# Reordering the start of an attention and MoE kernel: one w_in half ahead of V's last pair, reciprocals spread by TensorE, second tile's transposes and casts rearranged

## The chip, the cores and the metric

The kernel runs on one NeuronCore of a Trainium2 chip. The metric is the device time in microseconds (us); the span of the profile is some 1.8 us shorter than it. Ratios are the mean time of one kernel's fast runs over that of the kernel before in the same rounds, so they are not quite the ratios of the medians.

## The reference

```python
# attention in chunks of 64 keys: B = H = 8, S = 576, D = 64
scores = (1/sqrt(D)) * q_c @ k_c.T          # within each chunk
attn   = softmax(scores)
out    = attn @ v_c
# MoE: x is the attention's output as 4608 x 512
g   = gelu_exact(x @ w_in)                  # 512 x 2048
out = g @ w_out                             # 2048 x 512
```

## The kernel before

The 4608 tokens are worked in nine tiles of 512. A tile's attention (T: transposes of q and k, S: scores, U: sums and reciprocals, A: the product with V, called AV, and x = AV times reciprocal; each in four pairs of heads, 0 to 3) lies inside the matmuls of the tile ahead of it: the h products (x w_in, followed by Gelu) and then the y products (with w_out). From the second tile on, U is one step for all four pairs: sums on TensorE, a transpose and reciprocals on VectorE, 16 small copies on ScalarE (rb), then one more transpose per pair. Only the first tile has nothing in front of it. The start is therefore written out by hand, in the order in which each engine's queue gets its work:

```python
        load_v(0)                                             # eight transfers of 128 KB
        win = [load_w_in(c, 2 if c == 0 else 1) for c in range(NWC - 1)]
        # ... casts of q, k; all eight casts of V on GpSimd (PO); transposes; scores ...
        u2 = att_sum(0, 2, later=True)      # sum on TensorE, transpose, reciprocal, transpose on VectorE
        p3 = att_sum_pe(0, 3)               # sum and reciprocal small; p3() spreads it by 16 f32 matmuls
        u2()
        A[0]()
        p3()
        A[1]()
        act_table(Act.Gelu)
        keep_warm(1)
        A[2]()
        keep_warm(1)
        A[3]()
        # ...
        for i, eng in enumerate((PO, PO, DV, PO)):            # the first w_in quarter's four casts
            win[0](i, eng)
```

The spread:

```python
        def spread():
            rc_ps = ps_mm.tile([P, MT], f32, tag="mm", name="rc_ps")
            for m in range(MT // P):
                for r in range(2):
                    nc.tensor.matmul(rc_ps[CH * r:CH * (r + 1), m * P:(m + 1) * P],
                                     rr[:, m, r:r + 1].to_broadcast([P, D]), ident_f[:], ...)
            nc.scalar.copy(rc[:].rearrange("p n e -> p (n e)"), rc_ps[:])
```

The second tile's attention lies in the 16 slots of the first tile's second product (y = h w_out, four matmuls per slot):

```python
        for c in range(2, NWC):
            for i in range(FC):
                wout[c](i, PO)                                # GpSimd casts of w_out, then of V
        # ...
        phase(0, {}, {0: [lambda: act_table(Act.Exp)],
                      3: [T[0]], 4: [T[2]], 5: [T[4]], 6: [T[6], T[1]], 7: [T[3]], 8: [T[5], S_[0]], 9: [T[7], S_[1], next_qk],
                      10: [S_[2], S_[3]], 11: [U[0], lambda: act_table(Act.Gelu)], 12: [U[1], A[0]], 13: [U[2], A[1]],
                      14: [U[3], A[2]], 15: [U[4], A[3]]}, halved=True)
```

Even T are q, odd T are k. Slot 8 is the first to need the third quarter of w_out.

The softmax here doesn't subtract the row's maximum and nothing guards it: scores larger than these inputs give would overflow.

## Time and profile before

| | before |
|---|---|
| time, median of 3 runs at first | 296.86 us (296.45 to 296.9) |
| span of the profile | 294.0 us |
| TensorE busy | 281.9 us, 96% |
| first h product of tile 1 | 17.8 us |
| first h product of tile 2 | 52.0 us |

A TensorE that is 96% busy leaves 12 us at most. By the stretches, 6.6 us of it lie before 53 us, 3.8 us in the last stage and the end, and no more than 0.5 us in any stage between. The change touches only the first part. The lines are in the prediction. The profile is of a run of 295.75 us, 1.1 us below the median of the three.

### The profile page before, as it was taken

How to read it: one execution, taken by the hardware profiler on the slowest of the kernel's cores; microseconds unless marked ns; L12 is line 12 of the kernel's file. 1: busy time of each engine (PE TensorE's matmuls, PEld its weight loads, DVE VectorE, ACT ScalarE, POOL GpSimd, SP SyncE). 2: the span in 40 equal slices, each digit the busy share in tenths (PEclk: the TensorE clock that was granted, in tenths of full speed). 3: DMA queues.
4: the chain of work that ended last, by engine and by line, in shares of the span. 5: the costliest groups of instructions: out<-in, count | busy, mean ns of one | idle time of the engine just before them, and what ended most of it. 6: DMA issues, size and time to landing. Idle time of an engine off the chain costs nothing.

```text
span 294.0 us, 4846 instructions
## 1 busy us (share of the span) xinstructions
PE 281.9 (96%) x1837; PEld 138.2 (47%) x1871; DVE 126.5 (43%) x201; ACT 177.1 (60%) x380; POOL 98.6 (34%) x138
## 2 busy tenths in 40 slices
PE   5799999999999999999999999999999999999995
PEld 2554453345544454445445544554454445444444
DVE  6877256261816081618251735163325432550011
ACT  3756667767746773676368637872686368637400
POOL 7859748508711640182006500650003800000000
PEclk9999999999999999999999999999999999999999
DMA  7999999899669615971497149903999760020032
GB/s 231 272 377 404 393 271 291 272 210 331 172 166 323 161 68 149 314 183 71 130 300 204 58 136 287 248 36 124 206 127 150 223 143 2 36 88 21 0 71 71
DMA packets 96359, 53.79 MB, mean 183 GB/s; under 512 B 68560, under 2 KB 88272, under 8 KB 96336
## 3 DMA queue, kind: packets, MB, share of 16 engines
q1 hardware_dynamic: 96176, 53.36, 66.3%
q8 instruction: 14, 0.23, 0.3%
q10 hardware_dynamic: 160, 0.13, 0.2%
q14 instruction: 9, 0.07, 0.1%
HBM read 36.70 MB, written 9.44 MB: 157 GB/s over the span
## 4 chain that ended last, share of the span: by engine, by line
PE 81%; DMA 7%; SPq 4%; POOL 3%; ACT 2%; issue 1%; DVE 1%
PE h_ps L293 37%; PE y_ps L310 37%; DMA arrival<-in_moe_w_out_dram 4%; DMA arrival<-in_moe_w_in_dram 3%; PE av_ps L261 2%; PE s_ps L178 2%; SPq L127 2%; SPq L112 1%; PE y_ps L328 1%; ACT rb L225 1%; POOL w_in_sb L373 1%; PE sums_ps L216 1%; POOL w_out_sb L381 1%; POOL v_bd L462 1%; ACT y_sb L314 0%
## 5 line engine op out<-in xcount | busy, mean ns | idle before, releaser
L310 PE MATMUL y_ps<-w_out_sb,h 128*128 128x512 bf16 x539 | 130.5, 379 | 1.0
L293 PE MATMUL h_ps<-x,w_in_sb 128*128 128x512 bf16 x564 | 125.8, 379 | 1.6 <-ACT h L296 0.3
L296 ACT ACTIVATE h<-h_ps 128x512 bf16<-128x512 f32 x144 | 85.7, 597 | 63.6 <-PE h_ps L293 63.5
L293 PEld LDWEIGHTS <-w_in_sb 128*128 128x128 bf16 x576 | 56.3, 98 | 69.6 <-issue 1.8
L310 PEld LDWEIGHTS <-h 128*128 128x128 bf16 x560 | 49.6, 98 | 50.0 <-issue 1.8
L170 DVE COPY k_bd<-k_t 64x512 bf16<-64x512 bf16 x56 | 35.6, 635 | 48.0 <-DMA k_t<-k_nat 47.0
L131 POOL CAST q_nat<-arrival 128x512 bf16<-128x512 f32 x32 | 20.9, 692 | 95.2 <-DMA arrival<-in_q_dram 69.0
L135 POOL CAST v_bd<-arrival 64x512 bf16<-64x512 f32 (+1 forms) x30 | 36.5, 1216 | 20.3 <-DMA arrival<-in_v_dram 11.4
L225 ACT COPY rb<-r 32x16 f32<-32x16 f32 x128 | 25.8, 202 | 16.2 <-DVE r L221 14.5
L314 DVE COPY y_sb<-y_ps 128x512 f32<-128x512 f32 x17 | 11.7, 687 | 36.9 <-PE y_ps L310 36.9
L219 DVE STREAM_TRANSPOSE t<-sums_ps 128x512 f32<-128x512 f32 x8 | 5.7, 718 | 50.3 <-PE sums_ps L216 50.3
L262 DVE TENSOR_TENSOR x<-av_ps,rc 128x512 bf16<-128x512 f32 x36 | 24.7, 690 | 3.4
L232 DVE STREAM_TRANSPOSE rc<-rb 128x512 f32<-128x512 f32 x32 | 22.5, 704 | 7.3 <-ACT rb L225 7.3
L397 ACT ACT_TABLE_LOAD x18 | 23.1, 1283 | 1.0 <-PEq L520 0.7
L131 POOL CAST k_nat<-arrival 128x512 bf16<-128x512 f32 x32 | 18.6, 618 | 11.6 <-DMA arrival<-in_k_dram 5.7
L261 PEld LDWEIGHTS <-v_bd 128*128 128x128 bf16 x288 | 12.8, 98 | 9.5 <-POOL v_bd L135 2.5
L314 ACT COPY y_sb<-y_ps 128x512 f32<-128x512 f32 x18 | 10.2, 588 | 8.4 <-PE y_ps L310 8.4
L261 PE MATMUL av_ps<-pT,v_bd 128*128 128x64 bf16 x288 | 14.3, 193 | 0.6 <-POOL v_bd L135 0.3
L181 ACT ACTIVATE pT<-s_ps 128x512 bf16<-128x512 f32 x28 | 14.7, 592 | 0.0
L178 PEld LDWEIGHTS <-k_bd 128*128 128x128 bf16 x224 | 10.4, 98 | 6.6
L178 PE MATMUL s_ps<-q_t,k_bd 128*128 128x64 bf16 x224 | 11.1, 193 | 0.0
L155 ACT COPY k_bd<-tp 64x512 bf16<-64x512 bf16 x12 | 6.9, 579 | 4.8 <-PE tp L142 4.7
(59 smaller groups left out, 104.7 us busy)
## 6 DMA issues: line engine op xcount, KB each, us to landing
arrival<-in_v_dram SPq DMA_DIRECT2D x72, 128.0 KB, 4.1
out_dram<-y_sb SPq DMA_DIRECT2D x32, 256.0 KB, 2.0
arrival<-in_q_dram SPq DMA_DIRECT2D x7, 1024.0 KB, 6.1
arrival<-in_k_dram SPq DMA_DIRECT2D x7, 1024.0 KB, 8.5
arrival<-in_moe_w_out_dram SPq DMA_DIRECT2D x4, 1024.0 KB, 12.8
arrival<-in_moe_w_in_dram SPq DMA_DIRECT2D x3, 1024.0 KB, 10.4
arrival<-in_q_dram SPq DMA_DIRECT2D x4, 256.0 KB, 3.9
arrival<-in_k_dram SPq DMA_DIRECT2D x4, 256.0 KB, 4.4
```

Of the source, the lines that this page charges most:

```text
L131: copy(st[nm][:, g].rearrange("p j r d -> p r j d"), st[nm + "f"][:, 2 * g:2 * g + 2])
L135: copy(v_bds[t % NV][sl, :, gs, sl].rearrange("p i g d -> p g i d"), tiles[t]["vf"][sl, gs])
L170: copy(k_bds[g][sl, :, sl].rearrange("p i (c j) -> p i c j", j=J), src[sl])
L178: nc.tensor.matmul(s_ps[:, i, :].rearrange("p (j c) -> p j c", j=J), k_bds[g][:, i, :], qt[:, i], start=True, stop=True)
L225: nc.scalar.copy(rb[QD * s:QD * (s + 1), g], r1[QD * g:QD * (g + 1), s // 2])
L232: nc.vector.transpose(rc[:], rb[:, g].to_broadcast([P, NB, 32]))
L261: nc.tensor.matmul(av_ps[:, i, :], v_bds[t % NV][:, i, g, :], st["pT", g][:, i, :], start=True, stop=True)
L262: nc.vector.tensor_tensor(st["x"][:, g, :], av_ps[:].rearrange("p i e -> p (i e)"), st["rc", g][:].rearrange("p n e -> p (n e)"), op=mybir ...
L293: nc.tensor.matmul(h_ps[a][:], w_in_sb[:, ks, (f + a) * P:(f + a + 1) * P], st["x"][:, ks, :], start=(ks == 0), stop=(ks == KS - 1))
L296: nc.scalar.activation(st["h"][:, f + a, :], h_ps[a][:], Act.Gelu)
L310: nc.tensor.matmul(y_ps[:], st["h"][:, f, ms * P:(ms + 1) * P], w_out_sb[:, f, :], start=(f == 0), stop=(f == FF - 1))
L397: nc.scalar.activation(act_scratch[:], rest[:, 0:1], func)
```

## The change

Its intent: let the first w_in half land earlier, since GpSimd waits for it; take pair 2's two transposes off VectorE; let the second tile's k transposes start earlier; and share casts between GpSimd and VectorE.

```diff
-        load_v(0)
-        win = [load_w_in(c, 2 if c == 0 else 1) for c in range(NWC - 1)]
+        load_v(0, range(G - 1))
+        win = [load_w_in(0, lambda: load_v(0, [G - 1])), *[load_w_in(c) for c in range(1, NWC - 1)]]
 ...
-        for g in range(G):
+        for g in range(G - 1):
             cast_v(0, 0, PO, slice(g, g + 1))
             cast_v(0, 1, PO, slice(g, g + 1))
+        for i in range(2):
+            win[0](i, PO)
+        cast_v(0, 0, PO, slice(G - 1, G))
 ...
-        u2 = att_sum(0, 2, later=True)
+        p2 = att_sum_pe(0, 2)
         p3 = att_sum_pe(0, 3)
-        u2()
         A[0]()
+        p2()
+        A[1]()
         p3()
-        A[1]()
         act_table(Act.Gelu)
         keep_warm(1)
         A[2]()
+        cast_v(0, 1, DV, slice(G - 1, G))
         keep_warm(1)
         A[3]()
 ...
-        for i, eng in enumerate((PO, PO, DV, PO)):
-            win[0](i, eng)
+        win[0](2, PO)
+        win[0](3, PO)
 ...   (GpSimd casts only the first two of w_out's last quarter)
-                      3: [T[0]], 4: [T[2]], 5: [T[4]], 6: [T[6], T[1]], 7: [T[3]], 8: [T[5], S_[0]], 9: [T[7], S_[1], next_qk],
+                      3: [T[0]], 4: [T[2]], 5: [T[4], T[6]], 6: [T[1], T[3]], 8: [T[5], S_[0]],
+                      9: [T[7], lambda: wout[3](2, DV), lambda: wout[3](3, DV), S_[1], next_qk],
```

More of the change, by code (lines that the diff above doesn't have):

```diff
@@ L117, in load_qk, with load_v @@
                     src[b, h0:h1, MT:S, :].rearrange("h (p j) d -> p h j d", j=J))
-    def load_v(t, rs=(0, 1)):
-        vf = tiles[t]["vf"] = stage_tile()[:].rearrange("p (g i d) -> p g i d", g=G, d=D)
-        for g in range(G):
-            for r in rs:
+    def load_v(t, gs=range(G)):
+        if "vf" not in tiles[t]:
+            tiles[t]["vf"] = stage_tile()[:].rearrange("p (g i d) -> p g i d", g=G, d=D)
+        vf = tiles[t]["vf"]
+        for g in gs:
+            for r in range(2):
                 if t < B:
@@ L364, with load_w_in @@
     FC = FF // NWC
-    def load_w_in(c, parts=1):
+    def load_w_in(c, between=None):
         raw = stage_tile()[:].rearrange("p (ks n) -> p ks n", ks=KS)
-        n = WC // parts
-        for a in range(parts):
-            nc.sync.dma_start(raw[:, :, a * n:(a + 1) * n], w_in_v[:, :, c * WC + a * n:c * WC + (a + 1) * n])
+        n = WC // (2 if between else 1)
+        for a in range(0, WC, n):
+            nc.sync.dma_start(raw[:, :, a:a + n], w_in_v[:, :, c * WC + a:c * WC + a + n])
+            if between and a == 0:
+                between()
         def cast(i, copy):
@@ L416 @@
         cast_qk(0, "k", 3, PO)
-        for g in range(G):
+        for g in range(G - 1):
             cast_v(0, 0, PO, slice(g, g + 1))
             cast_v(0, 1, PO, slice(g, g + 1))
+        for i in range(2):
+            win[0](i, PO)
+        cast_v(0, 0, PO, slice(G - 1, G))
         cast_qk(0, "q", 0, DV)
@@ L471 @@
             cast_qk(1, "k", g, DV)
-        for c in range(2, NWC):
-            for i in range(FC):
-                wout[c](i, PO)
+        for i in range(FC):
+            wout[2](i, PO)
+        for i in range(2):
+            wout[3](i, PO)
         for g in range(G):
```

## The prediction

> **What bounds the kernel now**
>
> I read the page first, then busy times by stretch, then the timeline of the first 18 us engine by engine, then the chain of waits from 41 to 54 us. Busy times by stretch (us; PE, PEld, DVE, ACT, POOL; granted clock, DMA share, GB/s):
>
> ```profile
> PE 281.9 (96%) x1837; PEld 138.2 (47%) x1871; DVE 126.5 (43%) x201; ACT 177.1 (60%) x380; POOL 98.6 (34%) x138
> ...
> 0.00:17.78 17.78, 12.69 (x126) 7.52 (x127) 14.07 (x27) 9.60 (x16) 13.50 (x35) 1.00 0.90 269
> 17.78:31.95 14.17, 13.89 (x62) 6.28 (x65) 9.44 (x13) 9.61 (x17) 11.44 (x13) 1.00 1.05 397
> 31.95:41.00 9.05, 9.00 (x70) 5.00 (x70) 3.23 (x7) 5.79 (x10) 4.96 (x10) 1.00 1.09 381
> 41.00:52.99 11.99, 10.77 (x96) 4.77 (x97) 7.60 (x13) 9.39 (x28) 9.54 (x17) 1.00 0.88 252
> 52.99:83.33 30.34, 29.88 (x192) 14.40 (x196) 12.20 (x21) 19.15 (x43) 14.86 (x17) 1.00 0.83 233
> ```
>
> TensorE is the bound. From 53 us on it has no idle left worth naming, and the change touches nothing there. So only two things can move the time: when the first tile's first h product starts (17.8 us), and how much TensorE loses between 41 and 53 us. Both lie in code that the diff edits. From 17.8 to 41 us the transfers run without a gap, at about 390 GB/s: what lands there is set by the order and number of the bytes.
>
> The start, on TensorE, VectorE and GpSimd (start, length, engine, instructions, idle before):
>
> ```profile
> 14.52 0.25 PE L240 MATMUL sT<-ones_r,pT 128*128 128x2 bf16 x4
> 14.64 0.39 PE L261 MATMUL av_ps<-pT,v_bd 128*128 128x64 bf16 x8
> 15.31 1.09 PE L249 MATMUL rc_ps<-ident_f,rr 128*64 128x128 f32 x16 [0.28 <-DVE rr L243]
> 16.33 0.41 PE L261 MATMUL av_ps<-pT,v_bd 128*128 128x64 bf16 x8
> 17.79 0.39 PE L293 MATMUL h_ps<-x,w_in_sb 128*128 128x512 bf16 x1
> 18.34 0.39 PE L293 MATMUL h_ps<-x,w_in_sb 128*128 128x512 bf16 x1 [0.17 <-POOL w_in_sb L373]
> ...
> 16.12 2.55 DVE L262 TENSOR_TENSOR x<-av_ps,rc 128x512 bf16<-128x512 f32 x4
> ...
> 17.12 1.91 POOL L373 CAST w_in_sb<-arrival 128x512 bf16<-128x512 f32 x3 [1.27 <-DMA arrival<-in_moe_w_in_dram]
> ```
>
> Here the reader sees that GpSimd was idle for 1.27 us until the first w_in half landed at 17.1, and that the h products wait for its casts. From 18.34 they run without a hole: the next stage starts at 31.95, which is 63 x 0.216 = 13.6 us later. One matmul earlier, 18.12, is thus the effective start of the 64.
>
> The chain of waits in 41 to 54 us (start, length, what):
>
> ```profile
> 40.97 0.57 POOL w_out_sb L381
> 41.54 0.04 issue
> 41.58 0.38 PE y_ps L310
> 41.96 0.24 PE tp L142 x4
> ...
> 43.67 0.41 PE s_ps L190 x8
> ...
> 44.94 0.44 PE sums_ps L216 x4
> ...
> 49.99 1.28 ACT L397
> ...
> 51.49 1.46 ACT y_sb L314 x3
> ```
>
> The second tile's first h product needs a PSUM bank that ScalarE frees with a y copy. ScalarE reaches that copy only after 16 small rb copies (3.44 us) and the Gelu table load, and it starts those when the sums of the second tile are there. So the sums (44.9) set the start of the next stage (52.0): 7.1 us, in which nothing but this chain counts.
>
> **What the Trainium skill says**
>
> "TensorE: Matmul & The Clock Gate", section "Step-by-step: what each phase is for": matmuls stay in program order and only weight loads are pulled ahead. The trace agrees (no matmul above is out of the kernel's order). Hence a late AV product holds every h product behind it, even with x and w ready.
>
> "DMA: Bandwidth & Descriptors", section "Queues, rings and completion order": each DMA engine consumes descriptors in ring order. The trace agrees: w_in half 1, issued at 11.3 behind V, landed 5.7 us later.
>
> "SBUF — State Buffer" gives VectorE and GpSimd a shared port pair, which it calls "Lock-allocated, exclusive, held for the full instruction" (section Terms). The trace fits: VectorE's 128x512 casts took 0.42 us where GpSimd was idle (at 36.6) and 0.72 us beside a GpSimd cast (at 18.58).
>
> "ScalarE: Activation LUTs", section "What ACT_TABLE_LOAD costs": 1283 ns. The trace has 1.28 us in both places where a table load matters here.
>
> **The change part by part**
>
> *1. w_in half ahead of V's last pair.* The half is issued two V transfers earlier, 2 x 0.65 = 1.3 us. I put its landing at 15.8 instead of 17.1, V's last pair at about 16.5 instead of 13.3. GpSimd finishes six V casts at 10.34 + 6 x 0.69 = 14.5, casts w_in 0 and 1 from 15.8 to 17.1, then half of V's last pair until 17.8. Taken alone the h products could start about 1 us earlier.
>
> *2. Pair 2's reciprocals by TensorE.* Removed from VectorE: two transposes and a reciprocal, 0.68 + 0.25 + 0.71 = 1.64 us, just ahead of x. Added: a reciprocal of 0.17, a ScalarE copy of 0.59, and on TensorE 16 f32 products which take 1.02 us of its order (15.31 to 16.33 above) in place of one sum of about 0.22. The order becomes A0, spread 2, A1, spread 3, A2, A3. With pT for pair 3 at 14.5 as before: A0 at 14.64, spread 2 from 14.9, A1 at 15.9, spread 3 from 16.15 to 17.15, a warming product, A2 at 17.4. Without any other wait A3 comes at 17.8 and h at 18.0, practically the old 18.12. So part 2 uses up what part 1 wins.
>
> *3. Half of V's last pair on VectorE, behind x of pair 2.* This is the step that decides. x 2 needs A2, whose results stand at 17.8, and takes 0.64: 18.45. Then the V cast, 0.43 to 0.75 depending on GpSimd's w_in casts at that time: 18.9 to 19.2. A3 waits for it, and h waits for A3, 0.05 for the semaphore and 0.24 for eight products: 19.2 to 19.5. x of pair 3 follows by 20.4, in time for its use nine matmuls after the start. Against 18.12 the stage starts 1.1 to 1.4 us later; I take 1.2.
>
> *4. Second tile.* The transposes keep their order and only move between slots: q of pair 3 one slot up, k of pair 1 one slot up. The last ones, k of pairs 2 and 3, stay in slots 8 and 9, so the product that leads to the sums is preceded by the same TensorE work. Packing them may cost 0.1, since k of pair 1 needs a PSUM buffer whose ScalarE copy (0.59 each, two in a row) is just ending. In slot 8 the old kernel lost 0.2 waiting for the w_out cast of 40.97 (the fourth y product of the slot came at 41.58 instead of 41.38); a stage that arrives 1.2 later doesn't lose it. Sums: +1.2 + 0.1 - 0.2 = +1.1.
>
> *5. Two w_out casts to VectorE.* GpSimd is freed of 2 x 0.57, so its eight V casts begin at 44.1 instead of 45.2. Today each AV waits for them (0.3 to 0.8 us of weight-load idle at each). But behind those waits stands the ScalarE chain, which ends at sums + 7.1 whatever TensorE does, so I book nothing. The two casts on VectorE (0.43 to 0.83 each) fit between its last k copy and the sums' transpose: 43.61 to 45.40, a gap of 1.79.
>
> Sum: about +1.1 us at the start of the second tile, and the rest unchanged: 296.86 + 1.1 = 298.0. I go a little below, 297.6, because every timing of part 3 is a sum of small pieces and a faster result is easier to imagine than a much slower one.
>
> **The rivals**
>
> *The start wins.* If V's last pair lands before 16 us and A2 comes earlier than I think, x 2 and the V cast finish by 17.8; h starts at about 17.6, 0.5 earlier. For it: GpSimd's 1.27 us idle is real, and VectorE loses 1.6 us of work. Against it: spreads 2 and 3 stand in TensorE's order before A2. Even then the w_out transfer that lands at 39.18 holds slot 8 (casts until 41.53), so little of it reaches the sums: 296.4 to 296.9.
>
> *The V casts are the real bound of 41 to 53 us.* If the freed GpSimd lets AV and the y products end 1 us earlier and ScalarE's queue follows, the second stage gains up to 1 us: 296.0 to 297.0. Against it: the rb copies run back to back from 46.54 to 49.98 with no wait on TensorE.
>
> *A transfer starves.* V's staging buffer is released near 19.2 instead of 15.9, and a w_out load waits for it. Against it: at 19 us some 8.4 MB are issued and, by the GB/s row, some 5.2 MB moved; 3.2 MB at 0.39 MB/us is an 8 us reserve. If I am wrong, w_out lands later and the loss is 1 to 3 us: 299 to 300.
>
> **Range and chances**
>
> Loss at the start 0 to 1.5 and gain in the second stage 0 to 1 give 296.1 to 298.9 for 8 in 10. A 2% change is 5.9 us, as much as a third of the whole start; no mechanism here is that large. Faster 0.01, same 0.97, slower 0.02.
>
> **What would show it**
>
> Right: the w_in casts start near 15.8; A3's weight load waits for a VectorE v_bd cast at about 19; the first h product at 19.2 to 19.5; sums near 46; ScalarE's rb copies and table load in the chain as before; from 53 us on an unchanged profile, shifted. Wrong: A3 not waiting for VectorE, h before 18.2, or ScalarE's y copies starting other than 6.5 us after the sums. The size would be wrong if x 2 starts before 17.5 or if the f32 spreads take other than 1.02 us each.

## More of the kernel before

The rounds of different experiments fell on different chips at different times; the kernel before had medians of 296.44, 296.79, 297.24 and 296.68 us in them. Kernels of different rounds are therefore compared by their ratios.

## The result, and the profile after

The changed kernel took 298.25 us (median of 6 runs, 297.3 to 298.97) against 296.44 (6 runs, 295.66 to 296.9): a ratio of 1.0062, with a 95% interval of 1.004 to 1.0085. It is 1.8 us slower, which is within 2%.

TensorE's timeline of the changed kernel's start, then VectorE's and GpSimd's (start, length, engine, instructions, idle before):

```profile
13.32 0.61 PE L192 MATMUL s_ps<-qT,k_bd 128*128 128x64 bf16 x8 [0.59 <-ACT k_bd L157]
...
14.75 0.59 PE L263 MATMUL av_ps<-pT,v_bd 128*128 128x64 bf16 x8
15.27 1.98 PE L251 MATMUL rc_ps<-ident_f,rr 128*64 128x128 f32 x16
17.18 0.49 PE L263 MATMUL av_ps<-pT,v_bd 128*128 128x64 bf16 x8
17.60 1.09 PE L251 MATMUL rc_ps<-ident_f,rr 128*64 128x128 f32 x16
...
18.85 0.40 PE L263 MATMUL av_ps<-pT,v_bd 128*128 128x64 bf16 x8
...
20.65 0.39 PE L263 MATMUL av_ps<-pT,v_bd 128*128 128x64 bf16 x8 [1.18 <-DVE v_bd L137]
20.88 0.38 PE L295 MATMUL h_ps<-x,w_in_sb 128*128 128x512 bf16 x1
...
19.36 0.69 DVE L264 TENSOR_TENSOR x<-av_ps,rc 128x512 bf16<-128x512 f32 x1 [0.96 <-ACT rc L255]
20.08 0.42 DVE L137 CAST v_bd<-arrival 64x512 bf16<-64x512 f32 x1
...
15.70 1.16 POOL L377 CAST w_in_sb<-arrival 128x512 bf16<-128x512 f32 x2 [1.20 <-DMA arrival<-in_moe_w_in_dram]
```

The w_in casts do start 1.42 us earlier (15.70 for 17.12). They are of no use. A0, spread 2, A1, spread 3, A2 stand in line on TensorE. A3 then waits 1.18 us for VectorE's V cast, which itself stands behind x of pair 2. The h products begin at 20.88, where 19.2 to 19.5 had been forecast.

A second sight is the length of equal work. Spread 2 took 1.98 us and spread 3 only 1.09; the scores' eight matmuls took 0.61 us here and 0.41 at the same place in the kernel before. TensorE was at half rate until about 17.2 us here, and only until 13.4 there.

The chain of waits further on (start, length, what):

```profile
46.55 0.86 PE y_ps L312 x4
47.41 0.44 PE sums_ps L218 x4
...
52.46 1.28 ACT L401
...
53.96 1.46 ACT y_sb L316 x3
...
55.46 1.90 PE h_ps L295 x8
```

The sums come at 47.4 instead of 44.9, and from there the chain has the length that it had before. Busy times by stretch (the same columns as in the prediction):

```profile
20.88:34.69 13.81, 13.81 (x70) 6.27 (x67) 9.13 (x11) 8.84 (x15) 11.23 (x13) 1.00 1.06 397
34.69:43.47 8.78, 8.78 (x70) 5.00 (x69) 2.81 (x6) 5.58 (x10) 4.55 (x8) 1.00 0.98 320
43.47:55.46 11.99, 10.55 (x103) 5.18 (x100) 8.78 (x14) 9.52 (x28) 8.86 (x15) 1.00 0.77 232
55.46:85.80 30.34, 30.09 (x197) 14.38 (x197) 12.18 (x21) 19.14 (x43) 13.38 (x16) 1.00 0.83 233
```

The last cuts were laid at the distances that they had in the kernel before (11.99 and 30.34), so that their lengths show nothing. What does is the events: from the sums to the next tile's first h product it is 7.15 us before (44.87 to 52.02) and 7.14 here (47.34 to 54.48), and by TensorE's timeline the third tile's first h product comes at 82.90 before and at 85.36 here, 2.46 us later; the sums were 2.47 later. What was lost was lost before the sums.

### The profile page after: what moved, and what is told of

It reads as the page before. It is cut to its first block, busy times and chain, and to the rows that moved or that the text cites. A ratio compares the mean times of both kernels' runs of the same rounds, so it can differ in the third digit from the quotient of the medians.

```text
span 296.4 us, 4921 instructions
## 1 busy us (share of the span) xinstructions
PE 285.5 (96%) x1890; PEld 141.0 (48%) x1890; DVE 125.8 (42%) x201; ACT 177.6 (60%) x381; POOL 96.9 (33%) x136
## 2 busy tenths in 40 slices
DMA packets 96360, 53.81 MB, mean 182 GB/s; under 512 B 68560, under 2 KB 88272, under 8 KB 96336
## 4 chain that ended last, share of the span: by engine, by line
PE 91%; ACT 4%; DVE 3%; issue 1%
PE h_ps L295 42%; PE y_ps L312 39%; PE av_ps L263 3%; PE s_ps L180 2%; PE y_ps L330 1%; PE tp L144 1%; ACT k_bd L157 1%; ACT rb L227 1%; PE rc_ps L251 1%; PE sums_ps L218 1%; PE s_ps L192 1%; ACT y_sb L316 0%; DVE k_bd L157 0%; ACT L401 0%; DVE q_nat L133 0%
## 5 line engine op out<-in xcount | busy, mean ns | idle before, releaser
L312 PE MATMUL y_ps<-w_out_sb,h 128*128 128x512 bf16 x560 | 133.6, 379 | 0.0
L137 POOL CAST v_bd<-arrival 64x512 bf16<-64x512 f32 (+1 forms) x29 | 35.8, 1235 | 20.9 <-PE h_ps L295 11.2
L263 PE MATMUL av_ps<-pT,v_bd 128*128 128x64 bf16 x288 | 14.6, 195 | 1.9 <-DVE v_bd L137 1.2
L316 ACT COPY y_sb<-y_ps 128x512 f32<-128x512 f32 x18 | 10.2, 586 | 8.4 <-PE y_ps L312 8.4
```

The source lines that it names most:

```text
L137: copy(v_bds[t % NV][sl, :, gs, sl].rearrange("p i g d -> p g i d"), tiles[t]["vf"][sl, gs])
L263: nc.tensor.matmul(av_ps[:, i, :], v_bds[t % NV][:, i, g, :], st["pT", g][:, i, :], start=True, stop=True)
L312: nc.tensor.matmul(y_ps[:], st["h"][:, f, ms * P:(ms + 1) * P], w_out_sb[:, f, :], start=(f == 0), stop=(f == FF - 1))
```

## What fourteen profiles have in common

The profiles of the two kernels and of the twelve experiments can be put into one table. "S" is the start of the scores of pair 3 in tile 1, with their length in brackets: 0.41 is full rate, 0.61 half rate. "w_out" is the start of GpSimd's casts for slot 8, which had been waiting for that transfer each time. All numbers are us, each from its kernel's timeline. A profile is of one run and need not be a typical one: those of e5, e7 and e8 are of the slowest run of their kernel, those of e0, e3 and e9 of the fastest. So spans are not compared here, but distances within a profile.

| profile | S | first h | S to h | w_out | sums, tile 2 | first h, tile 2 | span |
|---|---|---|---|---|---|---|---|
| before | 13.41 (0.41) | 17.79 | 4.38 | 39.24 | 44.87 | 52.02 | 294.0 |
| changed | 13.32 (0.61) | 20.88 | 7.56 | 39.92 | 47.34 | 54.48 | 296.4 |
| e0 changed, again | 14.31 (0.41) | 20.50 | 6.19 | 40.52 | 46.96 | 54.11 | 296.1 |
| e1 V cast earlier | 14.49 (0.61) | 20.79 | 6.30 | 41.91 | 47.54 | 54.69 | 296.6 |
| e2 pair 2 on VectorE | 13.86 (0.61) | 20.92 | 7.06 | 39.93 | 47.39 | 54.53 | 296.5 |
| e3 start only | 13.97 (0.41) | 20.26 | 6.29 | 41.07 | 46.71 | 53.86 | 295.8 |
| e4 second tile only | 14.09 (0.41) | 18.15 | 4.06 | 41.03 | 46.66 | 53.81 | 295.8 |
| e5 changed, table late | 14.18 (0.61) | 21.55 | 7.37 | 40.99 | 48.02 | 54.63 | 296.0 |
| e6 before, table late | 13.43 (0.61) | 18.62 | 5.19 | 39.59 | 45.22 | 53.55 | 295.0 |
| e7 e1 and e2 together | 14.18 (0.41) | 19.55 | 5.37 | 43.42 | 49.05 | 56.19 | 298.1 |
| e8 e4, table late | 14.39 (0.61) | 19.73 | 5.34 | 41.00 | 46.63 | 53.24 | 294.8 |
| e9 e8, sums a slot earlier | 13.49 (0.61) | 18.86 | 5.37 | 39.54 | 44.79 | 51.46 | 293.1 |
| e10 changed, warmer | 12.83 (0.41) | 20.57 | 7.74 | 41.02 | 47.04 | 54.19 | 296.1 |
| e11 spread 2 only | 14.56 (0.41) | 19.41 | 4.85 | 41.07 | 46.70 | 53.84 | 295.8 |

Three things can be read from it.

**The sums come at whichever is later: first h + 26.46 or w_out + 5.63.** In the changed kernel, e0, e2, e5 and e10 the first holds to 0.02 us (20.88 + 26.46 = 47.34; 20.50 + 26.46 = 46.96). In before, e1, e4, e6, e7, e8 and e11 the second does (39.24 + 5.63 = 44.87; 43.42 + 5.63 = 49.05). In e3 both are equal within 0.02. Only e9, which moves the sums, has its own number (first h + 25.93). So a late start is hidden as far as the w_out landing is late. This landing wandered from profile to profile, between 39.2 and 41.1 with the old start and between 39.9 and 43.4 with the new order of transfers. The means are 40.2 and 41.1 (40.8 without e7); whether the new order delays it can't be said from so few, and no run tested it. Before slot 8 the transfers ran without a gap at 394 to 401 GB/s from 24 to 40 us; what differed was the time from 8 to 17 us, where they moved 217 to 284 GB/s, and in e7 also that from 17 to 24 us (321 GB/s, the others 369 to 400).

**The rate of TensorE rose by chance early or late.** Six profiles without e10 have full rate at S (it rose between 12.8 and 14.6), seven don't and rise between 17 and 19 us. Both groups hold kernels with the old start and with the new one. The same kernel fell in both (changed, late; e0, early). "TensorE: Matmul & The Clock Gate", section "What's actually happening", tells of a window of 3413 ns that is free-running, so that it does not begin with the kernel; the two groups lie about such a window apart. A late rise costs either start about as much: S to h is 4.06 to 4.38 at early rise and 5.19 to 5.37 at late rise with the old start (before, e4; e6, e8, e9), 6.19 to 6.29 and 7.37 to 7.56 with the new one (e0, e3; e5, changed).

**Like for like, the new start takes 2.0 to 2.2 us longer.** From the means of those groups: 6.24 - 4.22 = 2.0 at early rise, 7.47 - 5.30 = 2.2 at late rise. So the half rate is not the cause of the loss, though comparing one profile with one would have made it seem so. The old start at early rise, from the TensorE timeline of e4 (scores, third AV and fourth AV, h), to be set beside e0 below:

```profile
14.09 0.41 PE L190 MATMUL s_ps<-qT,k_bd 128*128 128x64 bf16 x8 [0.64 <-ACT k_bd L155]
...
17.47 0.40 PE L261 MATMUL av_ps<-pT,v_bd 128*128 128x64 bf16 x8
...
17.92 0.40 PE L261 MATMUL av_ps<-pT,v_bd 128*128 128x64 bf16 x8
18.15 3.62 PE L293 MATMUL h_ps<-x,w_in_sb 128*128 128x512 bf16 x15
```

Here h follows A3 at once, and so it does in e6, e8, e9 and e11. Of the six profiles with the old order of transfers only the first one had h waiting for w_in.

## The experiments

**e1: the V cast behind x of pair 1.** Is it the cast's place in VectorE's queue that holds A3, or the transfer?

```diff
         A[1]()
+        cast_v(0, 1, DV, slice(G - 1, G))
         p3()
 ...
         A[2]()
-        cast_v(0, 1, DV, slice(G - 1, G))
```

> The changed kernel with VectorE's V cast moved from behind x of pair 2 to behind x of pair 1; nothing else. Theory 1 (the cast's place in VectorE's queue holds A3): A3 follows A2 directly at about 19.3 in the changed kernel's clock phase, the first h product comes 1.2 to 1.5 us earlier than its 20.9, and the time falls by 0.9 to 1.3 us, to 297.0 to 297.3. Rival (the late landing of V's last pair holds A3): VectorE then waits for the transfer and h and the time stay within 0.3 us of the changed kernel's 298.25.

Measured: 297.66 us, ratio 1.0029 (0.9992 to 1.0066), about 1 us less than the changed kernel's 1.0062, as theory 1 had it (the median itself lies above its 297.0 to 297.3, but so did the kernel before's in these rounds). In its TensorE and VectorE timelines A3 (the third line below) follows the warming product at once:

```profile
20.11 0.40 PE L263 MATMUL av_ps<-pT,v_bd 128*128 128x64 bf16 x8 [0.16 <-POOL w_in_sb L377]
20.34 0.38 PE L396 MATMUL warm<-rest,ident 128*128 128x512 bf16 x1
20.56 0.40 PE L263 MATMUL av_ps<-pT,v_bd 128*128 128x64 bf16 x8
20.79 2.54 PE L295 MATMUL h_ps<-x,w_in_sb 128*128 128x512 bf16 x11
...
19.68 0.57 DVE L137 CAST v_bd<-arrival 64x512 bf16<-64x512 f32 x1
```

The first line is A2. The cast is done at 20.25, before A2 ends. S to h is 6.30 against 7.37 to 7.56 at the same (late) rise: 1.2 us, as theory 1 said. What is left over the old start's 5.19 to 5.37 is 1.0 us, and spread 2 still stands there. That the first h stands at 20.79 all the same is because S stands 1.2 us later in this profile (14.49 for 13.32). The interval of the ratio is wide and overlaps that of the changed kernel; the trace carries the verdict.

**e2: pair 2's reciprocals back on VectorE**, with the V cast left behind x of pair 2.

```diff
-        p2 = att_sum_pe(0, 2)
+        u2 = att_sum(0, 2, later=True)
         p3 = att_sum_pe(0, 3)
+        u2()
         A[0]()
-        p2()
-        A[1]()
         p3()
+        A[1]()
```

> The changed kernel with pair 2's reciprocals back on VectorE as before; the V cast stays behind x of pair 2. Theory 1 (spread 2 costs TensorE's order 1.0 us at full clock, 1.9 at half clock, and A2 stands behind it): A2 comes 1.0 to 1.9 us earlier, x of pair 2 and the V cast with it, so h starts 0.9 to 1.9 earlier and the time falls by 0.6 to 1.6 us, to 296.7 to 297.6. Rival (VectorE's 1.6 us of transposes were the bound of the start, so giving them back costs): h starts later or equal and the time is 298.2 or more.

Measured: 297.92 us, ratio 1.0040 (1.0015 to 1.0066), so 0.65 us less than the changed kernel, at the low end of what theory 1 allowed. The two intervals overlap, so the time alone does not bring the rival down; the trace speaks against it, and e11 below does. In the trace A2 comes 0.9 us earlier after S (18.49 - 13.86 = 4.63 against 5.53), but only 0.5 of it reaches h: x of pair 1 now waits behind the one spread that is left, at half rate 1.88 us, and the V cast still stands behind x of pair 2 (A3 waited 1.59 us for it).

**e3: the changed start with the old second tile**, and **e4: the old start with the changed second tile.** The edits swap the block of w_out casts and the slot table shown above.

> The changed start alone, with the second tile as before. Theory 1 (all of the loss is in the start; the second tile's part is worth 0 to 0.4): 298.2 to 298.7, and sums of the second tile at start of h plus 26.3 to 26.9 as in both kernels. Rival (the second tile's part gains about 1 us, or loses): 299 or more, or 297.5 or less.

> The second tile's changes alone, with the start as before. Theory 1 (ScalarE's chain behind the sums is the bound there, the freed GpSimd is of no use): 296.2 to 296.7, within 0.3 us of before; AV products no longer wait for GpSimd's V casts, yet h of the second tile starts 7.1 us after the sums as before. Rival (the V casts were the bound): 295.3 to 295.9, h less than 6.5 us after the sums.

Measured: e3 299.03 us, ratio 1.0080 (1.0052 to 1.0108), 0.3 us above what was expected and by its number in the rival's range (299 or more), though the kernel before was 0.35 us higher in these rounds too; e4 296.98 us, ratio 1.0007 (0.9978 to 1.0035). The loss lies in the start, and the second tile's part alone moves nothing that can be measured. In e4 first h minus sums is 53.81 - 46.66 = 7.15 us, the same as before. That no AV product would wait for GpSimd did not come true there: its last w_out quarter was cast from 44.89 on, and the weight loads of all four AV products wait for V casts, 1.7 us in sum (2.5 before). In the changed kernel and in e0 none does, and there too h comes 7.14 and 7.15 us after the sums. Whether the second tile's part takes back a little of a late start (1.0080 for e3, 1.0062 and 1.0052 for the whole change) can't be said within these intervals.

**e0: the changed kernel again**, as a control for the next three.

> The changed kernel once more, unaltered, as a control beside the next three and as a second profile of its start. Theory 1 (the loss is in the changed start, on average 1.2 to 2 us): 0.4 to 0.7% above before. What the profiles so far suggest besides: the matmuls change from 0.61 to 0.40 us (groups of eight 128x64) at a time that differs from run to run, 13.4 to 14.0 in some and 17.2 to 18.8 in others, and w_out for slot 8 lands between 39.2 and 41.9. If that is chance and not the change, this profile may show any of these, with spread 2 at 1.0 us when the rise is early and 1.9 when late.

Measured: 298.97 us, ratio 1.0052 (1.0026 to 1.0078). Its profile fell in the early rise. From its TensorE timeline:

```profile
14.31 0.41 PE L192 MATMUL s_ps<-qT,k_bd 128*128 128x64 bf16 x8 [0.59 <-ACT k_bd L157]
15.53 0.39 PE L263 MATMUL av_ps<-pT,v_bd 128*128 128x64 bf16 x8
15.86 1.09 PE L251 MATMUL rc_ps<-ident_f,rr 128*64 128x128 f32 x16
16.88 0.41 PE L263 MATMUL av_ps<-pT,v_bd 128*128 128x64 bf16 x8
17.22 1.09 PE L251 MATMUL rc_ps<-ident_f,rr 128*64 128x128 f32 x16
18.47 0.40 PE L263 MATMUL av_ps<-pT,v_bd 128*128 128x64 bf16 x8
20.27 0.39 PE L263 MATMUL av_ps<-pT,v_bd 128*128 128x64 bf16 x8 [1.18 <-DVE v_bd L137]
```

This is the prediction's order with its durations: 1.02 us from spread to the next AV (15.86 to 16.88), and the wait of A3 for VectorE. Only the whole lies 0.9 us later, because S does.

**e7: e1 and e2 together**, so that of the new start only the transfer order and the shared casts are left.

> The changed kernel with pair 2's reciprocals on VectorE as before and the V cast behind x of pair 1; left of the changed start are the transfer order and the shared V and w_in casts. Theory 1 (A3 late through spread 2 and the V cast, nothing else): the whole loss of the start is gone, within 0.3 us of before (0.999 to 1.001). Rival (the transfer order itself costs, because the second w_in half lands later or V's last pair holds A3): 0.6 us or more above before.

Measured: 297.76 us, ratio 1.0029 (0.9998 to 1.006). A miss: 0.9 us were left, where theory 1 had none and the rival 0.6 or more. In its TensorE and GpSimd timelines:

```profile
19.31 0.41 PE L263 MATMUL av_ps<-pT,v_bd 128*128 128x64 bf16 x8 [1.14 <-POOL v_bd L137]
...
17.34 1.17 POOL L377 CAST w_in_sb<-arrival 128x512 bf16<-128x512 f32 x2 [1.75 <-DMA arrival<-in_moe_w_in_dram]
18.45 0.80 POOL L137 CAST v_bd<-arrival 64x512 bf16<-64x512 f32 x1
```

A3 now waits 1.14 us for the other half of V's last pair. GpSimd's queue has it behind the two w_in casts, and these wait for w_in, which in this run landed at 17.3. In the other profiles with the new order where the casts were read they start between 15.0 and 17.3. So the new order carries a second wait of its own: A3 needs what stands behind w_in in one queue. Where w_in lands as in the changed kernel (that V cast done at 17.4) it would be hidden, by estimate. This profile is of the slowest of e7's six runs, 2.15 us above their median, and its w_out landed last of all; so how much of the 0.9 us this wait is on average stays open.

**e11: the kernel before with spread 2 only.** The edit is the reverse of e2's, in the old kernel.

> The kernel before with pair 2's reciprocals spread by TensorE and nothing else. Theory 1 (the spread takes 1.0 us of TensorE's order at full clock and 1.7 to 1.9 at half clock, and stands before A2 and A3): h of the first tile starts 0.3 to 1.0 us later than before's 17.8 to 18.6; after what the w_out landing of slot 8 hides, 0.1 to 0.8 us slower, ratio 1.000 to 1.003. Rival (VectorE's freed 1.6 us let x and h come earlier): ratio 0.999 or less.

Measured: 297.35 us, ratio 1.0025 (1.0007 to 1.0043), a loss of 0.7 us. S to h is 4.85 against 4.06 and 4.38. So spread 2 costs by itself, and the 1.6 us that VectorE wins bring no gain. The way from this start to the time is not shown by this profile: its sums came with w_out (41.07 + 5.63 = 46.70), and its first h had 0.8 us of slack.

**e5 and e6: the Gelu table load behind the third y copy**, in the changed kernel and in the one before.

```diff
-  11: [U[0], lambda: act_table(Act.Gelu)], ... 15: [U[4], A[3]]}
+  11: [U[0]], ... 15: [lambda: act_table(Act.Gelu), U[4], A[3]]}
```

> The changed kernel with the Gelu table load moved from behind the rb copies to behind the third y copy, so that the y copies no longer wait 1.3 us for it. Theory 1 (in 41 to 53 us ScalarE's chain is the bound, GpSimd's V casts are not): the y copies start at once after the rb copies, h of the second tile starts about 6.0 to 6.7 us after the sums in place of 7.1, and the time falls by 0.5 to 1.2 us against the changed kernel. Rival (TensorE's own AV and y order, paced by VectorE's x, is equally long): no more than 0.3 us.

> The kernel before with the same move of the table load. Theory 1: here the AV products are paced by GpSimd's V casts until 51.8, so the freed chain gives less than in the changed kernel: 0.3 to 0.8 us below before, h of the second tile starting about 6.7 to 7.0 us after the sums. If it gains as much as the changed kernel does or more, the V casts were no bound there either.

Measured: e5 296.37 us, ratio 0.9971 (0.9948 to 0.9994), against 1.0052 for the changed kernel in the same rounds, 2.4 us; e6 296.38 us, ratio 0.9965 (0.9943 to 0.9987), 1.0 us below before. ScalarE's timeline in e5:

```profile
49.69 3.43 ACT L227 COPY rb<-r 32x16 f32<-32x16 f32 x16 [1.83 <-DVE r L223]
53.14 1.56 ACT L316 COPY y_sb<-y_ps 128x512 f32<-128x512 f32 x3
54.72 1.28 ACT L401 ACT_TABLE_LOAD   x1
```

The copies follow at once, h starts 6.61 us after the sums, and the next h after the first three starts 9.61 us after the sums in place of 10.69 (58.03 - 47.34). That is 1.1 us, inside what was expected (0.5 to 1.2); the 2.4 us of the times are twice that. The other 1.3 of the 2.4 the profile doesn't show: it is of the slowest of e5's six runs, 1.55 us above their median. The two intervals allow for some of it, and the rest is open. In e6, TensorE's timeline shows what the prediction had left as a rival:

```profile
48.41 0.41 PE L261 MATMUL av_ps<-pT,v_bd 128*128 128x64 bf16 x8 [1.83 <-POOL v_bd L135]
```

GpSimd's V casts are the bound there, and h comes 8.33 us after the sums (53.55 - 45.22): in this run the last w_out quarter was cast only from 44.84 on (42.95 in the profile before), and V stood behind it. That is not owed to the table's move alone: with the old chain h would have come at 45.22 + 7.15 = 52.37, which is earlier still. So GpSimd's V casts hold the stage where that quarter lands late, and ScalarE's chain where it doesn't. Both numbers of e6 lie outside what was expected (0.3 to 0.8 us, h 6.7 to 7.0 us after the sums), and by which way its 1.0 us came about this one profile doesn't show.

**e10: five more warming products in the changed kernel's first 9 us.**

```diff
-        keep_warm(4)
+        keep_warm(6)
 ...     T[1]()
-        keep_warm(1)
+        keep_warm(2)
 ...     cast_qk(0, "q", 2, DV)
+        keep_warm(1)
         T[4]()
+        keep_warm(1)
```

> The changed kernel with five more warming products in TensorE's gaps up to 9 us. Theory 1 (the matmuls' change from half to full rate comes after a stretch of enough work, and by chance of its phase before or after spread 2): here it comes before 12 us in the profile, S of the last pair and spread 2 run at full rate (0.4 and 1.0 us), and the time falls by 0.2 to 0.8 us against the changed kernel, to a ratio of 1.002 to 1.004. Rival (the rate has no part in the loss): ratio 1.005 or more even with spread 2 at 1.0 us.

Measured: 297.85 us, ratio 1.0029 (1.0002 to 1.0056). Its ratio lies where theory 1 had it, but the condition for that did not come about, so it doesn't decide: the rate rose earlier, at about 8 us, but fell again at the first spread. From its TensorE timeline, and its busy times by stretch (granted clock third from the end):

```profile
14.38 1.72 PE L251 MATMUL rc_ps<-ident_f,rr 128*64 128x128 f32 x16
16.03 0.61 PE L263 MATMUL av_ps<-pT,v_bd 128*128 128x64 bf16 x8
16.57 1.82 PE L251 MATMUL rc_ps<-ident_f,rr 128*64 128x128 f32 x16
...
8.00:14.30 6.30, 4.23 (x63) 2.48 (x60) 5.28 (x12) 5.31 (x10) 5.44 (x9) 1.00 1.08 279
14.30:18.40 4.10, 4.10 (x47) 3.45 (x43) 1.52 (x3) 0.58 (x1) 1.83 (x4) 0.58 0.97 311
```

At full rate the same groups take less time, TensorE was then busy 1.94 of 3.20 us between 10.2 and 13.4, and the mean clock over both spreads was 0.58. What a start at full rate throughout would give is left open.

**e8: the old start, the changed second tile and the late table load; e9: the same, with T5, T7, the scores and the sums one slot earlier** (slots 7, 8, 9 and 10, the two shared w_out casts behind the sums).

> Start of before, second tile of the changed kernel, and the table load behind the third y copy. Theory 1 (the freed GpSimd is worth something as soon as ScalarE's chain is shorter): faster than the kernel before with the table move alone, which had 0.9965: 0.991 to 0.995, some 295. No A product waits for GpSimd's V casts; h starts 6.6 us after the sums. Rival (the second tile's part is worthless in any company): 0.996 to 0.998.

> As the last, with the k transposes of pairs 2 and 3 and all scores one slot earlier and the sums one slot earlier (slot 10 instead of 11), the two shared w_out casts behind them. Theory 1 (the sums start the chain that ends the stage, and slot 8's w_out landing holds what stands behind it): the sums come about 1 us earlier relative to the y products and no longer wait for that landing, another 0.3 to 1.0 us: 0.988 to 0.993. If V casts or TensorE's order are the bound by then, no more than 0.2.

Measured: e8 295.86 us, ratio 0.9976 (0.9957 to 0.9996); e9 295.73 us, ratio 0.9966 (0.9945 to 0.9986). Both beat the two kernels; neither is shown to beat e6 with its one moved line, and both are short of what was expected; e8 lies where its rival had it. In e8 h is 6.61 us after the sums, but that no AV product would wait for GpSimd did not come true. From the waits of its weight loads (us in total, times, longest):

```profile
PEld L261 <- POOL v_bd L135: 2.3, 4, 0.6
```

VectorE's x of pair 1, for which the last AV product waits in e4, ended at the same time as the last V cast (52.09 and 52.07), so that the last AV product had two bounds at once. Of the 1 us by which e9 should move the sums only 0.5 is left: they come 25.93 us after the first h in place of 26.46. A transpose now waits 0.16 us for ScalarE's copy of k, which it did not in the others; the rest is not explained.

## Why the prediction was right or wrong

The prediction's direction and its cause hold: 297.6 was forecast, 298.25 measured, inside 296.1 to 298.9. The size was too small: the sum of its parts was a loss of 1.1 us, which was then lowered to 0.7, and 1.8 was measured.

*Step 1, w_in half ahead:* right in the landing: the casts start at 15.70, forecast 15.8. (The 5.7 us that the prediction names for the old landing are one transfer's time and show no order by themselves.) The gain of about 1 us that it booked for this was not there: it was read off a profile in which w_in landed last, and in the five other profiles with the old order h waits for A3 and not for w_in. The order on GpSimd was foreseen, but not that V's last pair becomes a wait when w_in lands late (e7).

*Step 2, spread 2:* right as a mechanism and in its duration at full rate, 1.02 us (e0). The term was taken from a profile in which the rate had risen early; in the changed kernel's own profile it was 1.91 us (15.27 to 17.18), one of the signs that the prediction had named for a wrong size. Alone it costs 0.7 us of time (e11), where the prediction let it cancel the w_in gain.

*Step 3, the V cast behind x of pair 2:* right. A3 waits 1.18 us for VectorE in the changed kernel, e0, e5 and e10, and moving the cast takes 1.2 us out of the start (e1). The size of the term "I take 1.2" was off. Like for like the start lost 2.0 to 2.2 us. A part of the gap is the yardstick: the first h of the profile before stood 4.38 us behind S (4.71 by the effective start that the prediction used) because w_in landed last, and in e4 the same start had 4.06. The rest is 0.3 us of small pieces in TensorE's order (S to h of 6.2 where 5.9 was forecast).

*Step 4, the slots:* the transposes' moves change nothing that e4 could measure (0.9978 to 1.0035). The term "-0.2" for slot 8 was too small. By the rule of the table the old start had slack of 0.6 us at slot 8 in the profile before (44.87 - 17.79 - 26.46), or 0.3 from its effective start, and of 0.1, 0.4 and 2.1 in e6, e8 and e4. So 2.1 lost at the start, less the slack of 0.3 to 0.8 (0.8 is the mean of those four), leaves 1.3 to 1.8, and 1.5 to 1.8 were measured (1.0052 and 1.0062). That the two wrong sizes partly cancelled was luck.

*Step 5, casts to VectorE:* right that nothing could be booked: e4 is at 1.0007, and from sums to h it was 7.14 to 7.15 us with either second tile, as long as the table load stayed in its place.

*The rivals:* "the start wins" fell with e11 and the traces. "The V casts are the real bound" is false in every profile with the table load in its old place, and true in e6's, where the last w_out quarter landed late. "A transfer starves" was not seen in the changed kernel: from 17 to 24 us the transfers ran at 398 GB/s before and 392 after, from 24 to 40 us at 397 in both. The 321 GB/s of e7 between 17 and 24 us are not explained.

## What to carry to other kernels

An engine that works in order makes every early arrival worthless if what stands in front of it in its queue comes later: follow the queue of each engine up to the first product that matters, not the landing of its operand. Where two bounds run beside each other (here a transfer and TensorE's start), write down the rule for the later of them from several profiles; it tells how much of a delay is hidden. One profile's start is a draw: transfers and clock moved it by a microsecond in either kernel, so compare like with like before blaming the change.

## What the Trainium skill lacked or had wrong

- "TensorE: Matmul & The Clock Gate" (section "What's actually happening"): it says that about 3.4 us of sustained work release the full rate, but gives no share of busy time that counts as sustained. Here TensorE was busy 2.69 of 3.40 us (6.8 to 10.2, before) and the rate still rose only at 12.8 to 14.6 or at 17 to 19 us; and 1.94 of 3.20 us was followed by a fall (e10). 1.62 of the 2.69 us were transposes, which the page's Part 4 ("PE-mode transpose") says do not count as busy in the same way; no run here separates the two.
- The same page: it warns that the recorded events of the clock gate are unreliable, but has no case like this one: here the granted clock was blind to the first half-rate phase. The stretches up to 17 us show 1.00 in the changed kernel, while equal groups took 0.61 and 0.41 us; only the later fall in e10 shows, as 0.58.
- "ScalarE: Activation LUTs" (section "What ACT_TABLE_LOAD costs") adds a drain of some 1380 ns to each switch of tables. Here the load took its 1.28 us and no more: in the kernel before the last copy ends at 49.98, the load starts at 49.99, and the next instruction at 51.29.
- "DMA: Bandwidth & Descriptors": no page tells how much a kernel's first transfers differ between runs. Here they moved 217 to 284 GB/s between 8 and 17 us, and the third w_out quarter was there between 39.2 and 43.4 us.
